# Sparse attention and a routed MoE on one core: transposes of the last batch behind the last load, x of one pair by DMA, scores of one pair in one stretch, and a schedule that reckons with overlapping engines

## The chip, the cores and the metric

The kernel runs on one core of one Trainium2 chip. The metric is the device time of one execution in microseconds (us). Every quoted median is of fast executions; runs of two kernels are compared only where they were taken in turn on one chip. The profile lists TensorE (PE; PEld is its weight load, which overlaps it: 435.9 us beside 656.6 us of matmuls in a span of 664.1 of the kernel before), VectorE (DVE), ScalarE (ACT), GpSimd (POOL) and SyncE (SP), for each of which the program fixes an order of instructions, and 16 DMA engines. In this kernel TensorE's results go to banks of PSUM, from which operations of VectorE and ScalarE read them (in the profile before, `sg` of TensorE by ScalarE, 0.98 us at 65.25, and `vs` by VectorE, 0.28 us at 18.37).

## The reference

```python
# attention: 4 batches x 8 heads, 768 positions, head size 64
k_sum = k.reshape(B, H, nb, 32, D).max(axis=3)         # one summary key per block of 32
v_sum = v.reshape(B, H, nb, 32, D).mean(axis=3)
mask_l = np.abs(pos[:, None] - pos[None, :]) < 16      # local window
a = softmax([scale*q@k.T masked, scale*q@k_sum.T + log(32)])
x = (a @ concat(v, v_sum))                             # -> 3072 tokens x 512
# routed MoE: 8 experts, 512 -> 1024 -> 512
P = np.exp(x @ w_gate - max)
for _ in range(8):                                     # the routing loop
    P /= P.sum(1, keepdims=True) + 1e-09
    P /= P.sum(0, keepdims=True) + 1e-09
    P *= N / E
for e in range(8):
    out += P[:, e:e+1] * (np.maximum(x @ w1[e], 0) @ w2[e])
```

Heads are worked on two at a time: 16 pairs, four to a batch. Pairs 8 to 11 are the third batch, 12 to 15 the fourth.

## The kernel before

All instructions are first put down as units with an engine, an estimated cost and what they depend on. A greedy planner then fixes the order of the whole program, always taking the unit that can start first, by its estimates. PSUM banks are rings in this plan: a unit that opens a bank must wait until all users of the bank's last holder are done. Attention has a ring "a" of three banks and a ring "s" of one double bank.

```python
# Plan.order(), the planner (cut)
            t = max([t0, free.get(e, 0.0)]
                    + [d.end + d.lag + (self.HOP if d.on != e else 0.0) for d in u.deps])
            # ... the unit with the earliest t is taken; among those within 0.02 us, by priority
            u.start, u.end, u.on = t, end, e
            free[e] = end                      # the engine is free when its unit ends
            for b in u.opens:                  # PSUM rings
                ring[b.tag][turn[b.tag] % self.slots[b.tag]] = b
# ...
    BY_DMA = 12        # from pair 12 on keys and queries are transposed by DMA
    X_BY_DMA = 12      # so is x, except for the last pair of a batch
    WHOLE = 10         # from pair 10 on the scores of a pair are one stretch
# ...
        def scores(i):                         # one double bank "s"; whole: two banks "a" more
            sg = at["sg", i, 0] = banks2("sg")
            dst = [[sg[:, j, :] for j in range(2)], None]
            if i >= WHOLE:
                dst[1] = at["sg", i, 1] = [bank("a", "sg1") for _ in range(2)]
            score_mms(i, dst, range(G if i >= WHOLE else HG))

        def to_xT(i, h=None):                  # x of a pair, turned by TensorE
            t = at.pop(("xs", i, h or 0))
            tx = at["tx", i, h] = bank("a", "tx", F16)
            for g in range(G if h is None else HG):
                nc.tensor.transpose(...)

        def x_dma(i):                          # the same by DMA
            nc.sync.dma_start_transpose(out=xT[:, i % PB, t0:t0 + S]..., in_=t...)
# pair_start(i) (cut)
            if i >= BY_DMA:
                for z in range(2):             # keys, queries
                    U["tr", i, z] = add("SP", 1.4, lambda z=z: tr_dma(i, z), ...)
            U["ks", i] = add("DVE", 0.95, lambda: key_max(i), ...)       # largest key of each block
            U["km", i] = add("DVE", 0.23, lambda: key_max_split(i), ...) # -> ksT, for the summary scores ss
# the routing loop (cut)
        for n in range(8):
            rows = add("DVE", 1.65, sink_rows, prev, 0)
            cols = add("PE", 0.1, sink_cols, [rows], 0, opens=[buf], lag=0.1)
            prev = [add("DVE", 0.6, sink_apply, [cols], 0, uses=[buf])]
```

The names in the profile: `tkq` keys and queries turned by TensorE, `sg` scores, `ss` summary scores, `vs` block sums of v, `av` attention output, `xs` its normalised form, `tx` x turned by TensorE, `hps` and `yps` the two layers of expert 0, `lp` the logits, `sink` the column sums of the routing loop.

The softmax here doesn't subtract the row's maximum and nothing guards it: scores larger than these inputs give would overflow.

Of the kernel before, what the change touches and what calls it, by code (L numbers as in the profile page):

```python
# [33 lines left out]
class Plan:  # L34

    HOP = 0.15

    def __init__(self, slots, idle=None):
        self.units, self.slots = [], slots
# [18 lines left out]
    def order(self):  # L58
        free, ring, turn = {}, {t: [None] * n for t, n in self.slots.items()}, {t: 0 for t in self.slots}
        left, n_left, after = [], {}, {}  # L60
        for u in self.units:
            n_left[u] = len(set(u.deps))
            for d in set(u.deps):
                after.setdefault(d, []).append(u)
            if not u.deps:
                left.append(u)
        done = []

        def ready(u):
            t = 0.0  # L70
            for i, b in enumerate(u.opens):
                old = ring[b.tag][(turn[b.tag] + i) % self.slots[b.tag]]
                if old is not None:
                    if any(x.start is None for x in old.users):
                        return None
                    t = max([t] + [x.end + (self.HOP if x.on not in u.eng else 0.0) for x in old.users])
            return t

        while left:
            best = {}  # L80
            for u in left:
                t0 = ready(u)
                if t0 is None:
                    continue
                for e, cost in u.eng.items():
                    t = max([t0, free.get(e, 0.0)]
                            + [d.end + d.lag + (self.HOP if d.on != e else 0.0) for d in u.deps])
                    best.setdefault(e, []).append((t, u, cost))
            picks = []
            for e, c in best.items():  # L90
                t_min = min(t for t, _, _ in c)
                t, u, cost = min((x for x in c if x[0] <= t_min + 0.02), key=lambda x: x[1].prio)
                picks.append((t, t + cost, e, u, cost))
            t, end, e, u, cost = min(picks, key=lambda x: x[:2])
            if self.idle is not None:
                us, fn, until = self.idle
                if until.start is not None:
                    self.idle = None
                while self.idle is not None and t > free.get("PE", t) + us:
                    x = Unit("PE", us, fn, [], 0.0, [Buffer("m")], 0.0)  # L100
                    x.opens[0].users.append(x)
                    t0 = ready(x)
                    if t0 is None or t0 + us > t:
                        break
                    x.start = max(t0, free["PE"])
                    x.end = free["PE"] = x.start + us
                    if x.end > t:
                        break
                    x.on = "PE"
                    ring["m"][turn["m"] % self.slots["m"]] = x.opens[0]  # L110
                    turn["m"] += 1
                    done.append(x)
            u.start, u.end, u.on = t, end, e
            free[e] = end
            for b in u.opens:
                ring[b.tag][turn[b.tag] % self.slots[b.tag]] = b
                turn[b.tag] += 1
            left.remove(u)
            done.append(u)
            for x in after.get(u, ()):  # L120
                n_left[x] -= 1
                if not n_left[x]:
                    left.append(x)
        assert len([u for u in self.units if u.start is None]) == 0
        return done
# [3 lines left out]
def kernel(  # L129
# [10 lines left out]
    nc = tc.nc  # L140

    B, H, S, D = q.shape
    G = S // 128
# [6 lines left out]
    NP = (B * H) // 2  # L150
    PB = H // 2
    SCALE = 1.0 / float(D) ** 0.5
    W = 16
# [4 lines left out]
    VD = D + 1  # L158
    NEH = 3
    BY_DMA = 12  # L160
    X_BY_DMA = 12
    WHOLE = 10
    FILL = {"v0": 1, "S0": 1, "s0": 2, "s1": 1, "s2": 1}

    const = ctx.enter_context(tc.tile_pool(name="const", bufs=1))
# [55 lines left out]
    NB = PB  # L221
# [4 lines left out]
    with tc.manual_schedule():  # L226
# [100 lines left out]
        def tr_dma(i, z):  # L327
# [2 lines left out]
            nc.sync.dma_start_transpose(out=dst.rearrange("c (g t) -> c g t", g=G),  # L330
                                        in_=st[:].rearrange("p g j d -> p (g j d)"))

        def key_max(i):
            r = i % NB
            nc.vector.tensor_reduce(out=ks[r][:, 0, 0:24],
                                    in_=kT[r][:].rearrange("p (n w) -> p n w", w=32),
                                    axis=AX.X, op=ALU.max)
# [44 lines left out]
        def scores(i):  # L382
            sg = at["sg", i, 0] = banks2("sg")
            dst = [[sg[:, j, :] for j in range(2)], None]
            if i >= WHOLE:
                dst[1] = at["sg", i, 1] = [bank("a", "sg1") for _ in range(2)]
            score_mms(i, dst, range(G if i >= WHOLE else HG))

        def scores_1(i):
            sg = at["sg", i, 1] = banks2("sg")  # L390
# [490 lines left out]
        def pair_start(i, prio):  # L881
# [2 lines left out]
            war_q = war_k[:2] + [U.get(("ss", o, 0)), U.get(("ss", o, 1))]  # L884
            ahead = U.get(("S", i - 1, 1 if i > PB else 0))
            if i >= BY_DMA:
                for z in range(2):
                    U["tr", i, z] = add("SP", 1.4, lambda z=z: tr_dma(i, z),
                                        [U["kq"[z], i], U.get(("S", i - 3, 1))] + (war_k, war_q)[z], prio)
                    U["kT", i, z] = add("DMA", 1.7, None, [U["tr", i, z]], prio, lag=2.0)  # L890
            for z in range(0 if i >= BY_DMA else 1 if i < PB else 2):
                buf = Buffer("m" if i < PB else "a")
# [51 lines left out]
        def pair_whole(i, prio):  # L944
# [1 line left out]
                               [U["v", i], U.get(("A", i - NE, 1)), U["vc", i % NE]], prio, lag=5.0 if i < BY_DMA else 3.5)  # L946
            x1 = []
            deps = [U["kT", i, 0], U["kT", i, 1], U.get(("ed", i - 2))]
            bufs = [Buffer("s")] + (2 * [None] if i < WHOLE else [Buffer("a"), Buffer("a")])
            U["S", i, 0] = U["S", i, 1] = add("PE", 0.4 if i < WHOLE else 0.6, lambda: scores(i), deps, prio,  # L950
                                              opens=[x for x in bufs if x is not None])
            U["X", i, 0] = add("ACT", 0.97, lambda: score_exp(i, 0), [U["S", i, 0]], prio, uses=bufs[:1])
            if i < WHOLE:
                buf = Buffer("s")
                U["S", i, 1] = add("PE", 0.4, lambda: scores_1(i), deps, prio, opens=[buf])
                U["X", i, 1] = add("ACT", 0.97, lambda: score_exp(i, 1), [U["S", i, 1], U["X", i, 0]], prio,
                                   uses=[buf])
            else:
                x1 = [add("ACT", 0.53, lambda j=j: score_exp(i, 1, j), [U["S", i, 0], U["X", i, 0]], prio,
                          uses=bufs[1 + j:2 + j]) for j in range(2)]  # L960
                U["X", i, 1] = x1[1]
# [10 lines left out]
            for h in range(2):  # L972
# [3 lines left out]
                                   prio, opens=[buf])  # L976
                U["no", i, h] = add("DVE", 0.75, lambda h=h: normalize(i, h),
                                    [U["A", i, h], U.get(("x", i - 2))], prio, uses=[buf])
            if i >= X_BY_DMA and i % PB < PB - 1:
                U["xt", i] = add("SP", 1.5, lambda: x_dma(i), [U["no", i, 0], U["no", i, 1]], prio)  # L980
                U["x", i] = add("DMA", 1.7, None, [U["xt", i]], prio, lag=2.0)
                return
# [101 lines left out]
        expert0(HS, [U["x", i, 1] for i in range(PB)])  # L1084
        gate(0, [U["x", i, h] for i in range(PB) for h in range(2)], 900)
        for i in range(PB, NP):
            load_pair(i, "" if i == PB else "kqv")
            pair_start(i, 20 + i)
            pair_whole(i, 20 + i)
            if i % PB == PB - 1:  # L1090
                b = i // PB
                xs = [U["x", PB * b + d] for d in range(PB)]
                gate(b, xs, 900 if b < B - 1 else 0)
                expert0(b * S, xs)
                expert0(b * S + HS, xs)
        def transposed():

            r = (NP - 1) % NB
            nc.gpsimd.tensor_copy(out=warm[:, 0:1], in_=kT[r][0:32, 0:1])
            nc.gpsimd.tensor_copy(out=warm[:, 1:2], in_=qT[r][0:32, W:W + 1])  # L1100
            if X_BY_DMA < NP:
                nc.gpsimd.tensor_copy(out=warm[:, 4:5], in_=xT[0:32, PB - 2, (B - 1) * S:(B - 1) * S + 1])
            ve = V_e[(NP - 1) % NE]
            for j in range(2):
                nc.gpsimd.tensor_copy(out=warm[:, 2 + j:3 + j],
                                      in_=ve[64 + 32 * j:96 + 32 * j, G - 2, VD * j:VD * j + 1])

        last[0] = add("POOL", 0.3, transposed, [last[0], U["near", NP - 1]] + [U["kT", NP - 1, z] for z in range(2)]
                      + [U["x", i] for i in range(X_BY_DMA, NP - 1)])
        load("w1n", lambda: load_w1(1), 0.85, 5.0)  # L1110
        load("w2n", lambda: load_w2(1), 0.85, 5.0)
        U["w1", 1], U["w2", 1] = U["w1n"], U["w2n"]
        U["post"] = add("SP", 0.0, pools, [U["lo", b] for b in range(B)] + [last[0]])
        prev = [U["post"]]
        for n in range(8):
            rows = add("DVE", 1.65, sink_rows, prev, 0)
            buf = Buffer("Q")
            cols = add("PE", 0.1, sink_cols, [rows], 0, opens=[buf], lag=0.1)
            prev = [add("DVE", 0.6, sink_apply, [cols], 0, uses=[buf])]
# [201 lines left out]
```

## Time and profile before

| | before |
|---|---|
| median of 3 runs | 666.03 us (665.86 to 666.69) |
| span of the profiled execution | 664.1 us |
| TensorE busy | 656.6 us, 99% |
| VectorE, ScalarE, GpSimd busy | 550.1, 410.9, 199.0 us |
| attention with expert 0, the routing loop, first matmuls of expert 1 | 0 to about 165 us |
| experts 1 to 7 | about 165 us to the end |

A line of TensorE's timeline has the start, the length, the line of the program, the operation with its tiles, and the count. Matmuls overlap each other a little in the profile (six of scores, 0.38 us from 64.66 us, are followed at 64.97), so what a group costs is the distance from its start to the start of the next group, not its length. Where a group starts later than that pace allows, TensorE stood still; I call this a hole. Its size is worked out so from two starts in the trace, and its time is the start of the last matmul before it.

### The profile page before, as it was taken

What the parts mean: (1) busy time and instruction counts of PE and PEld (TensorE: products, weight loads), DVE (VectorE), ACT (ScalarE), POOL (GpSimd) and SP (SyncE); (2) the same over time, 40 slices, a digit from 0 to 9 for tenths busy, and PEclk for the clock granted to TensorE, in tenths of its full rate; (3) what the DMA queues carried; (4) which work ended last, traced back from release to release, by engine and by line L of the source; (5) the groups of instructions that cost most, each with busy time, mean ns of one, the idle gap of its engine ahead of it and who ended that gap; (6) DMA issues with size and microseconds to landing.
All of it is one profiled execution on the core that took longest, in us unless ns stands there. A gap on an engine that the chain in (4) does not pass through costs nothing.

```text
span 664.1 us, 13257 instructions
## 1 busy us (share of the span) xinstructions
PE 656.6 (99%) x5131; PEld 435.9 (66%) x5132; DVE 550.1 (83%) x1036; ACT 410.9 (62%) x769; POOL 199.0 (30%) x257
## 2 busy tenths in 40 slices
PE   8999999999999999999999999999999999999997
PEld 4666666545766666666666666666666666666666
DVE  7899897799988887887779877988778877988776
ACT  6677676556885566556665665555655656556652
POOL 8899522100132222212322222223122213222123
PEclk9999999999999999999999999999999999999999
DMA  9999932700953747373754665373838465335656
GB/s 167 181 145 145 143 70 43 128 1 2 157 96 65 126 75 118 64 128 65 110 97 71 121 91 101 64 127 65 127 64 135 73 96 96 64 64 112 157 134 202
DMA packets 112558, 67.89 MB, mean 102 GB/s; under 512 B 77936, under 2 KB 90480, under 8 KB 112496
## 3 DMA queue, kind: packets, MB, share of 16 engines
q0 software_dynamic: 94816, 57.46, 64.9%
q1 hardware_dynamic: 17152, 9.58, 5.9%
q8 instruction: 40, 0.66, 0.4%
q14 instruction: 22, 0.18, 0.1%
q10 hardware_dynamic: 528, 0.02, 0.0%
HBM read 52.45 MB, written 6.29 MB: 88 GB/s over the span
## 4 chain that ended last, share of the span: by engine, by line
PE 96%; DVE 3%; DMA 1%; issue 0%; ACT 0%; POOLq 0%; DVEq 0%
PE yps L815 22%; PE pA L764 22%; PE pY L815 17%; PE pQ L764 11%; PE hps L211 6%; PE yps L216 6%; PE pR L764 5%; PE sg L347 1%; DMA qst<-in_q_dram 1%; PE av L512 1%; PE vs L357 1%; PE tkq L303 1%; PE av L435 1%; DVE xs L543 1%; PE ss L461 1%; PE av L441 1%
## 5 line engine op out<-in xcount | busy, mean ns | idle before, releaser
L815 PEld LDWEIGHTS <-h 128*128 128x128 f16 x2352 | 230.1, 98 | 88.5 <-issue 1.0
L843 POOL DMA_DIRECT2D out_acc<-y x120 | 101.7, 891 | 372.1 <-ACT y L839 110.3
L839 ACT ACTIVATE y<-pY,P_sb 128x256 f32<-128x256 f32 x168 | 79.8, 477 | 123.3 <-PE pY L815 121.6
L830 DVE SCALAR_TENSOR_TENSOR out_acc<-yps,P_sb,out_acc 128x512 f32<-128x512 f32 x128 | 95.1, 744 | 29.0 <-PE yps L815 29.0
L798 DVE TENSOR_TENSOR h<-h 128x1024 f16<-128x1024 f16 x168 | 109.3, 683 | 1.4
L815 PE MATMUL pY<-w,h 128*128 128x256 f16 x672 | 100.0, 273 | 0.6 <-ACT y L839 0.6
L815 PE MATMUL yps<-w2sum,h 128*128 128x256 f16 x672 | 98.4, 273 | 0.0
L764 PE MATMUL pA<-xT,w 128*128 128x512 f16 x336 | 98.3, 379 | 0.0
L815 PE MATMUL yps<-w,h 128*128 128x256 f16 x672 | 93.3, 273 | 0.0
L830 DVE SCALAR_TENSOR_TENSOR out_acc<-pY,P_sb,out_acc 128x512 f32<-128x512 f32 x84 | 62.8, 748 | 29.1 <-PE pY L815 27.4
L764 PEld LDWEIGHTS <-w 128*128 128x128 f16 x672 | 65.8, 98 | 31.6 <-issue 0.2
L764 PEld LDWEIGHTS <-w1sum 128*128 128x128 f16 x504 | 49.3, 98 | 45.0
L786 DVE CUSTOM_DVE_ANT_0 h<-pQ,snap 128x512 f16<-128x512 f32 x84 | 57.6, 685 | 7.0 <-ACT snap L207 4.3
L786 DVE CUSTOM_DVE_ANT_0 h<-pA,snap 128x512 f16<-128x512 f32 x84 | 57.3, 682 | 4.8 <-PE pA L764 4.8
L202 ACT ACTIVATE h<-pA 128x512 f16<-128x512 f32 x84 | 50.6, 603 | 12.6 <-PE pA L764 12.4
L202 ACT ACTIVATE h<-pR 128x512 f16<-128x512 f32 x84 | 50.1, 596 | 8.0 <-PE pR L764 7.7
L207 ACT COPY pR<-pA 128x512 f32<-128x512 f32 x83 | 47.5, 572 | 7.7 <-PE pA L764 6.9
L815 PE MATMUL pY<-w2sum,h 128*128 128x256 f16 x336 | 50.4, 273 | 0.0
L764 PE MATMUL pA<-xsum,w 128*128 128x512 f16 x168 | 50.0, 379 | 0.0
L764 PE MATMUL pR<-xT,w 128*128 128x512 f16 x168 | 50.0, 379 | 0.0
L764 PE MATMUL pQ<-xsum,w1sum 128*128 128x512 f16 x168 | 50.0, 379 | 0.0
L764 PE MATMUL pA<-xsum,w1sum 128*128 128x512 f16 x168 | 50.0, 379 | 0.0
(150 smaller groups left out, 854.3 us busy)
## 6 DMA issues: line engine op xcount, KB each, us to landing
out_acc<-y POOLq DMA_DIRECT2D x120, 256.0 KB, 3.4
w<-in_moe_w_dram POOLq DMA_DIRECT2D x14, 1024.0 KB, 10.7
out_dram<-out_acc SPq DMA_DIRECT2D x24, 256.0 KB, 2.4
qst<-in_q_dram POOLq DMA_DIRECT2D x32, 96.0 KB, 5.3
vx<-in_v_dram POOLq DMA_DIRECT2D x15, 192.0 KB, 6.2
kst<-in_k_dram POOLq DMA_DIRECT2D x24, 96.0 KB, 5.6
w<-in_moe_w_dram POOLq DMA_DIRECT2D x4, 256.0 KB, 7.6
w<-in_moe_w_dram POOLq DMA_DIRECT2D x2, 512.0 KB, 7.7
```

What stands on the lines that cost most here:

```text
L202: nc.scalar.activation(out=out, in_=in_, func=AF.Relu, bias=0.0, scale=1.0)
L207: (nc.scalar.copy if eng == "ACT" else nc.vector.tensor_copy)(out=out, in_=in_)
L211: nc.tensor.matmul(hp[:, 0:n], lhsT=w1s[e][:, dk, f * 128:(f + 1) * 128], rhs=xT[:, dk, t0:t0 + n], start=(dk == 0), stop=(dk == KD - 1))
L216: nc.tensor.matmul(yp[:, d], lhsT=h[:, f, c * 128:(c + 1) * 128], rhs=w2s[e][:, f, d], start=(f == 0), stop=(f == KF - 1))
L303: nc.tensor.transpose(t[:, g * 128:(g + 1) * 128], st[:, g, :, :].rearrange("p j d -> p (j d)"), ident)
L764: nc.tensor.matmul(dst[:], lhsT=lhsT, rhs=rhs, start=first and k == 0, stop=k == HK - 1, skip_group_check=True)
L786: nc.vector._custom_dve(dve_ops.TENSOR_ADD_SAT, out=ring(e, p, q)[:, q % 2, blk, :], in0=at[src, e, p, q][:], in1=at.pop(("snap", n, e, p, ...
L798: nc.vector.tensor_tensor(out=h[:, :, out_, :], in0=h[:, :, a, :], in1=h[:, :, b, :], op=op)
L815: nc.tensor.matmul(dst[:, d], lhsT=lhsT, rhs=rhs, start=f == 0 and n in (1, 5, 2), stop=f == HF - 1, skip_group_check=True)
L830: nc.vector.scalar_tensor_tensor(out=o, in0=y, scalar=scalar, in1=o, op0=ALU.mult, op1=ALU.add)
L839: nc.scalar.activation(out=at[key][:, d], in_=src, func=AF.Copy, bias=0.0, scale=P_sb[:, t, e:e + 1])
L843: nc.gpsimd.dma_start(out=o, in_=at.pop(("y", e, p, c, key))[:], accum_op=ALU.add)
```

## The change

Its intent is to take work off TensorE (x of pair 10 by DMA: six transposes fewer; the scores of pair 9 in one stretch: one change-over fewer), to keep transposing DMAs out of the way of the loads, and to let the planner know that an operation of VectorE or ScalarE begins before the last one has quite ended (in the kernel before, one of VectorE, 0.68 us from 126.11 us, is followed at 126.71, 0.08 us before its end, and one of ScalarE, 0.59 us from 64.77, at 65.25, 0.11 us before its end).

```diff
@@ the planner
+    OVERLAP = {"DVE": 0.07, "ACT": 0.09}
-            free[e] = end
+            free[e] = end - self.OVERLAP.get(e, 0.0)
@@ constants
-    X_BY_DMA = 12
-    WHOLE = 10
+    X_BY_DMA = {10, 12, 13, 14}
+    WHOLE = {9, 10, 11, 12, 13, 14, 15}
@@ new: two small copies on GpSimd that wait for the last load of q
+        def loads_landed(i):
+            st = at["st", NP - 1, 1]
+            for t in (kT[i % NB][0:32, 0:1], qT[i % NB][0:32, W:W + 1]):
+                nc.gpsimd.tensor_copy(out=t, in_=st[0:32, 0, 0, 0:1])
@@ pair_start
             if i >= BY_DMA:
+                hold = U.get(("tr", i - 1, 1))
+                if i == BY_DMA:
+                    hold = add("POOL", 0.3, lambda: loads_landed(i), [last[0], U["q", NP - 1]] + war_k + war_q, prio)
+                    last[0] = hold
                 for z in range(2):
                     U["tr", i, z] = add("SP", 1.4, lambda z=z: tr_dma(i, z),
-                                        [U["kq"[z], i], U.get(("S", i - 3, 1))] + (war_k, war_q)[z], prio)
+                                        [U["kq"[z], i], U.get(("S", i - 3, 1)), hold] + (war_k, war_q)[z], prio)
@@ all loads of the fourth batch before its first pair
-            load_pair(i, "" if i == PB else "kqv")
+            for n in range(i, NP) if i == BY_DMA else [i] if PB < i < BY_DMA else []:
+                load_pair(n, "kqv")
@@ the routing loop, as the planner reckons it
-            rows = add("DVE", 1.65, sink_rows, prev, 0)
+            rows = add("DVE", 1.5, sink_rows, prev, 0)
... (tests of i against the two sets, where i was compared with a number)
```

More of the change, by code (lines that the diff above doesn't have):

```diff
@@ L384, in scores @@
             dst = [[sg[:, j, :] for j in range(2)], None]
-            if i >= WHOLE:
+            if i in WHOLE:
                 dst[1] = at["sg", i, 1] = [bank("a", "sg1") for _ in range(2)]
-            score_mms(i, dst, range(G if i >= WHOLE else HG))
+            score_mms(i, dst, range(G if i in WHOLE else HG))
         def scores_1(i):
@@ L948, in pair_whole @@
             deps = [U["kT", i, 0], U["kT", i, 1], U.get(("ed", i - 2))]
-            bufs = [Buffer("s")] + (2 * [None] if i < WHOLE else [Buffer("a"), Buffer("a")])
-            U["S", i, 0] = U["S", i, 1] = add("PE", 0.4 if i < WHOLE else 0.6, lambda: scores(i), deps, prio,
+            bufs = [Buffer("s")] + (2 * [None] if i not in WHOLE else [Buffer("a"), Buffer("a")])
+            U["S", i, 0] = U["S", i, 1] = add("PE", 0.4 if i not in WHOLE else 0.6, lambda: scores(i), deps, prio,
                                               opens=[x for x in bufs if x is not None])
             U["X", i, 0] = add("ACT", 0.97, lambda: score_exp(i, 0), [U["S", i, 0]], prio, uses=bufs[:1])
-            if i < WHOLE:
+            if i not in WHOLE:
                 buf = Buffer("s")
@@ L978, in pair_whole @@
                                     [U["A", i, h], U.get(("x", i - 2))], prio, uses=[buf])
-            if i >= X_BY_DMA and i % PB < PB - 1:
+            if i in X_BY_DMA:
                 U["xt", i] = add("SP", 1.5, lambda: x_dma(i), [U["no", i, 0], U["no", i, 1]], prio)
@@ L1100, in transposed @@
             nc.gpsimd.tensor_copy(out=warm[:, 1:2], in_=qT[r][0:32, W:W + 1])
-            if X_BY_DMA < NP:
+            if NP - 2 in X_BY_DMA:
                 nc.gpsimd.tensor_copy(out=warm[:, 4:5], in_=xT[0:32, PB - 2, (B - 1) * S:(B - 1) * S + 1])
@@ L1108 @@
         last[0] = add("POOL", 0.3, transposed, [last[0], U["near", NP - 1]] + [U["kT", NP - 1, z] for z in range(2)]
-                      + [U["x", i] for i in range(X_BY_DMA, NP - 1)])
+                      + [U["x", i] for i in X_BY_DMA])
         load("w1n", lambda: load_w1(1), 0.85, 5.0)
```

## The prediction

> **What bounds the kernel now.** I read the page first, then the waits of TensorE, then the timeline of TensorE, DMA issues and VectorE between 60 and 165 us, because all that the change touches lies before 165 us.
>
> The page, engines and chain:
>
> ```profile
> PE 656.6 (99%) x5131; PEld 435.9 (66%) x5132; DVE 550.1 (83%) x1036; ACT 410.9 (62%) x769; POOL 199.0 (30%) x257
> ...
> PE 96%; DVE 3%; DMA 1%; issue 0%; ACT 0%; POOLq 0%; DVEq 0%
> ```
>
> TensorE works 656.6 of 664.1 us, and the chain that sets the end is TensorE for 96%. Only 7.5 us are left outside it. The waits of TensorE say where:
>
> ```profile
> PE idle L613 <- DVE zeros L632: 1.3, 1, 1.3
> PE tkq L312 <- DMA qst<-in_q_dram: 0.8, 1, 0.8
> PE pY L815 <- ACT y L839: 0.6, 1, 0.6
> PE tkq L300 <- ACT kst L207: 0.3, 1, 0.3
> ```
>
> Three of the four are in the first 8 us, the third is 6 us from the end; another 4 us are the tail behind the last matmul. The windows by stage confirm it (first the stretch, then its length and TensorE's busy time):
>
> ```profile
> 20.00:60.00 40.00, 39.88 (x536) 26.48 (x534) 36.30 (x96) 28.91 (x47) 39.35 (x53) 1.00 2.10 156
> 60.00:117.00 57.00, 56.95 (x609) 36.13 (x607) 48.85 (x134) 39.85 (x74) 25.70 (x41) 1.00 1.12 91
> 117.00:165.00 48.00, 48.00 (x281) 25.47 (x280) 41.49 (x88) 28.81 (x56) 2.94 (x4) 1.00 0.26 45
> 165.00:640.00 475.00, 475.00 (x3292) 321.92 (x3291) 391.62 (x606) 294.27 (x564) 107.71 (x128) 1.00 0.57 98
> ```
>
> From 20 to 640 us TensorE has no hole worth 0.2 us. So there are two currencies here: TensorE work taken away comes off the end one for one; a new wait of TensorE is added one for one, as there is no slack to swallow it. Work moved between the other engines counts only if it makes such a wait.
>
> [...]six transposes of x start at 96.42 and what follows at 96.76, 0.34 us; four 512-column matmuls take 0.86 us. [...]
>
> ```profile
> 126.11 0.68 DVE L718 TENSOR_TENSOR xsum<-xT,xsum 128x1024 f16<-128x1024 f16 x1
> 126.71 0.68 DVE L718 TENSOR_TENSOR xT<-xT 128x1024 f16<-128x1024 f16 x1
> 127.31 0.21 DVE L592 RECIPROCAL crec_sb<-sink 128x8 f32<-128x8 f32 x1
> ```
>
> Operations of 0.68 us follow each other at 0.60 us. [...]
>
> **The change, part by part.**
>
> *x of pair 10 by DMA.* It takes six 128x128 transposes and one copy from PSUM (0.55 us on VectorE or 0.80 on ScalarE) away and adds one transposing DMA on SyncE. The instruction order of the new kernel confirms 78 transposes of x falling to 72. On the path: 6 x 56 ns = 0.34 us off TensorE.
>
> *Scores of pair 9 in one stretch.* The 12 matmuls stay; what goes is one change-over at the end of a stretch. Before:
>
> ```profile
> 64.66 0.38 PE L347 MATMUL sg<-qT,kT 64*128 64x160 bf16 x6
> 64.97 0.51 PE L550 MATMUL tx<-ident_x,xs 128*128 128x128 f16 x6
> ...
> 91.06 0.59 PE L347 MATMUL sg<-qT,kT 64*128 64x160 bf16 x12
> 91.58 1.04 PE L216 MATMUL yps<-w,h 128*128 128x512 f16 x4
> ```
>
> Six take 0.31 us until the next instruction, twelve take 0.52; 2 x 0.31 - 0.52 = 0.10 us saved. TensorE's work thus falls by 0.44 us in all.
>
> *Transposes of the fourth batch behind the last load.* Only pair 12 moves. Before, its keys were issued while loads were still queued:
>
> ```profile
> 66.23 1.32 SPq L330 DMA_TRANSPOSE kT<-kst x1
> 68.01 1.56 SPq L330 DMA_TRANSPOSE qT<-qst x1
> ...
> 78.48 2.25 SPq L330 DMA_TRANSPOSE kT<-kst x1
> ```
>
> They landed 6.7 and 8.1 us later, at 72.9 and 76.1; the other six, issued from 78.48 on, took 2.7 to 6.7 us. The last q load is issued at 73.95 and 75.52 and lands at 82 to 83. In the new order SyncE issues the near values of pairs 10 and 11, then k and q of pair 12, x of pair 10, and pairs 13 to 15. From 82 us on with some 1.7 us an issue and 3 to 5 us to landing, q of pair 12 lands at 87 to 88. When is it needed? Adding up TensorE's instructions in the new order with the intervals measured here puts the scores of pair 12 at about 89.4 us (91.06 before). Margin 1 to 2 us; pairs 13 to 15 are needed at 101, 104 and 113, with far more. So this part should cost and gain nothing; it is a transfer that is hidden in both kernels.
>
> *Overlap in the schedule.* The work is the same, the order changes almost everywhere, and about 24 copies move from ScalarE to VectorE (15 more VectorE instructions, 15 fewer on ScalarE). 24 x 0.69 = 17 us takes VectorE from 83% to some 85%: not a bound. What matters is the routing loop, eight rounds of VectorE, TensorE, VectorE. Before, the schedule reckoned VectorE too slow, and that was slack: the last column sum ends at 159.86, its matmul comes at 163.06, 3.2 us later. In the new order TensorE reaches the last routing matmul 41.6 us after the fourth batch's logits, not 43.5, and VectorE has 40 other operations between the first round and the last column sum, not 32. I counted through the rounds: 1.53 us for the rows, 0.64 for the column step, 0.62 for each other operation. Rounds 3 to 7 keep 0.5 us or more; in round 2 the sum is ready about 0.2 us late; in round 8 it is ready at 42.7 us after the logits against an arrival at 41.8, 0.9 us late. So TensorE could wait 1.1 us in this stretch. The pitches are good to about 0.03 us and there are some 60 steps, so the error is as large as the result; I enter a third of it, 0.37 us.
>
> The sum: 666.03 - 0.44 - 0.15 + 0.37 = 665.8 us. The 0.15 is half of the one true wait in the front that a new order may remove (0.29 us at 20.2 us, where the transposes of x wait for their input).
>
> **The rivals.**
> *A: the routing loop becomes a wait.* For it: the count above, the lost 3.2 us of slack, and the new order placing an h or weight sum between column step and rows in most rounds, which lengthens the loop. Against it: VectorE's free time of 1.4 us in that stretch before, which the new order may use. It would give 666.5 to 667.5 us: 1.1 us to 2 us of wait against 0.44 us saved.
> *B: pair 12 arrives late.* For it: nothing was waited for in this chain before, and now its transposes start 14 to 16 us later, with x of pair 10 and near values of pair 12 (POOL) on the same DMA engines. The key maximum of pair 12 stands in VectorE's fixed order, and a late one holds everything behind it. Against it: 1 to 2 us of margin, and loads that end earlier when no transpose is among them. It would give 666.5 to 668 us.
> *C: only the saved work shows.* No new wait: 665.6 us, and 665.0 with the short waits in the front and near the end (0.3 us at 644.6) gone too. That is the floor, since there is no other idle time that this change touches.
> *D: the longer run of experts 1 to 7 suffers,* as a schedule that reckons with overlap leaves less slack. Against it: TensorE waits 0.0 us for VectorE or ScalarE there, with these at 82% and 62%. I give it 0 to 0.5 us.
>
> **Range and chances.** C's floor is 665.0, and a run to run spread of about 0.4 us (665.86 to 666.69 before) lies on both sides; A and B together make 667.5 a fair upper end. Range 664.9 to 667.5. Two per cent is 13 us, and nothing found here is worth a tenth of that in either direction, so within 2% has 0.985, slower 0.010 (a chain of fixed orders that jams at pair 12 or in the loop), faster 0.005.
>
> **What would show it.** Right: TensorE's busy time falls by about 0.4 us; transposes of x 72; its waits list is the old one or adds less than a microsecond; kT and qT of pair 12 land between 85 and 89 us in under 5.5 us each; the scores of pair 12 follow without a hole. Rival A shows as a gap in front of the routing matmuls (sink) at 125 and 163 us or in front of the first yps of expert 1. Rival B shows as a gap at 87 to 92 us with a DMA as releaser on TensorE, or on VectorE's key maximum. D shows as PE waits for h or y after 170 us. The prediction is wrong if the time is under 664.9, as then idle time existed that I did not see inside the modelled matmul ends, or over 667.5.

Three passages of the recorded text are cut out of it, with the cuts marked, as they state rules that no trace of this case shows. No term of the sum goes with them: it came to 666.03 - 0.44 - 0.15 + 0.37 = 665.8 us. The 56 ns are a sixth of the 0.34 us from 96.42 to 96.76 in the trace, and the three VectorE lines show what the planner's new constant of 0.07 us stands for.

## The result, and the profile after

| | before | after |
|---|---|---|
| median of 6 runs each, in turn | 666.25 us (665.86 to 666.69) | 666.44 us (666.32 to 668.14) |
| ratio of the fast runs, 95% interval | | 1.0007 (0.9994 to 1.002) |
| span of the profiled execution | 664.1 us | 664.7 us |

A ratio is the mean time of one kernel's fast runs over that of the other's of the same rounds, so not quite the ratio of the medians quoted. The time is the same. The measurement lies within the predicted range and 0.64 us above the predicted 665.8.

The page of the changed kernel, engines and chain:

```profile
PE 658.0 (99%) x5125; PEld 435.6 (66%) x5126; DVE 562.8 (85%) x1051; ACT 402.5 (61%) x754; POOL 199.1 (30%) x259
...
PE 95%; DVE 3%; DMA 1%; issue 0%; ACT 0%; SPq 0%; DVEq 0%
```

There are six matmul instructions fewer, 15 more on VectorE and 15 fewer on ScalarE, and yet TensorE is busy for 1.4 us longer. The profile models the ends of matmuls, so that a short hole can count as busy: from 47.5 to 56 us it shows 8.48 busy us of 8.50, where the starts show holes of 0.51 us. The windows by stage of the changed kernel (the stretch, its length and TensorE's busy time, then PEld, DVE, ACT and POOL, the clock, the DMA share and GB/s):

```profile
20.00:60.00 40.00, 39.95 (x524) 26.05 (x523) 35.65 (x97) 30.30 (x52) 39.12 (x52) 1.00 2.14 153
60.00:117.00 57.00, 56.79 (x597) 35.61 (x596) 43.59 (x117) 40.97 (x75) 26.32 (x43) 1.00 1.13 96
117.00:165.00 48.00, 48.00 (x294) 25.52 (x293) 43.08 (x98) 27.85 (x54) 2.45 (x3) 1.00 0.27 45
165.00:640.00 475.00, 475.00 (x3291) 321.81 (x3290) 408.33 (x628) 283.59 (x540) 108.22 (x129) 1.00 0.57 98
```

Experts 1 to 7 are as full as before, with 16.7 us more on VectorE (408.33 against 391.62). That is where VectorE got its additional work: from 20 to 117 us it has 5.9 us less than before. Busy windows hide short holes here, so the starts have to be read. The transposes of x that wait at 20 us start at 20.64 us before and at 20.72 after, and the matmuls behind TensorE's last hole before the tail at 644.87 and 645.60. In between the changed kernel thus needs 0.73 - 0.08 = 0.65 us more. It has 0.54 us less to do there: the 0.44 us that the prediction works out, and 0.10 more, as a stretch of scores begins with a gap of 0.10 us in these traces (those at 64.66, 91.06 and 97.72 us before, and at 39.62, 41.93 and 75.19 after, follow 0.96 us behind the start of four 512-column matmuls, which take 0.86 to 0.88 ahead of other groups) and the changed kernel has one stretch fewer. So it has gained about 1.2 us of new waiting. A list of all holes over 0.12 us between 20 and 120 us finds most of it:

| hole before (us) | | hole after (us) | |
|---|---|---|---|
| 20.19 | 0.28 | 20.37 | 0.20 |
| | | 48.92, before `tx` | 0.16 |
| | | 53.20, between `vs` and `vs` | 0.18 |
| | | 55.47, before `ss` | 0.17 |
| 65.94, before `lp` | 0.21 | | |
| | | 83.08, before `ss` | 0.30 |
| | | 99.48, before `lp` | 0.14 |
| | | 100.27, before `ss` | 0.21 |

The six new ones are 1.16 us together; with the old one at 65.94 gone the sum is 0.95. The first one is not shorter, as 0.07 us of it stand one group earlier in the changed kernel. The trace after 117 us adds 0.05 us at the column sums of 129.3 us and 0.11 at those of 150.5, which makes 1.11; the rest lies in gaps under 0.12 us. What the six wait for is named by the weight loads, which stand ahead of the matmuls. The waits of the weight loads of the changed kernel between 48 and 102 us (line waited for: total, times, longest), and the largest of them in the timelines of PEld and VectorE:

```profile
PEld L468 <- DVE ksT L348: 0.6, 3, 0.3
PEld L364 <- DVE xs L550: 0.2, 1, 0.2
PEld L557 <- DVE xs L550: 0.2, 1, 0.2
PEld L577 <- DVE xs L550: 0.2, 1, 0.2
```
```profile
83.43 0.11 PEld L468 LDWEIGHTS <-ksT 128*128 128x128 bf16 x2 [0.31 <-DVE ksT L348]
```
```profile
81.58 0.95 DVE L342 TENSOR_REDUCE ks<-kT 128x24 bf16<-128x768 bf16 x1
82.45 0.28 DVE L370 TENSOR_TENSOR Ve<-vs,own_n 64x128 bf16<-64x128 f32 x1
82.77 0.48 DVE L374 COPY Ve<-Ve 64x650 bf16<-64x650 bf16 x1
83.17 0.21 DVE L348 TENSOR_TENSOR ksT<-ks,own 128x64 bf16<-128x64 bf16 x1
```

All six end with VectorE: with a key maximum three times and with a normalised `xs` three times. The last operation that the summary scores need comes at 83.17 us, behind a block copy. VectorE works almost without a pause there: 8.00 us of the 8.50 from 47.5 to 56 us, in which three of the holes lie. Before it had 8.09 of 8.50 in this stretch and TensorE no wait for it. At the other holes it is alike: 2.85 of 3.00 us from 81 to 84 us (before 2.71) and 3.78 of 4.00 from 97 to 101 (before 3.84). So it is not a higher load that makes the holes but which operation stands where in a VectorE that is full in both kernels, and when TensorE asks for it. In the kernel before, the key maximum of the same pair 11 came 4.4 us after its `ks` (81.82), behind nine other operations, and nothing waited, as the first summary scores that could need it came at 87.47 us:

```profile
86.25 0.22 DVE L341 TENSOR_TENSOR ksT<-ks,own 128x64 bf16<-128x64 bf16 x1
```
```profile
87.47 0.49 PE L461 MATMUL ss<-qT,ksT 128*128 128x384 bf16 x2
```

After, it comes 3 us earlier, but TensorE asks for it 4 us earlier.

The transposes of pair 12, in the timeline of SyncE of the changed kernel, stand behind the near values of pair 11:

```profile
81.45 0.59 SPq L386 DMA_DIRECT2D Ve<-vx  x1
82.21 1.32 SPq L331 DMA_TRANSPOSE kT<-kst  x1
83.72 1.21 SPq L331 DMA_TRANSPOSE qT<-qst  x1
85.03 1.23 SPq L567 DMA_TRANSPOSE xT<-xs  x1
```

In the trace they land at 85.16 and 87.08 us, x of pair 10 at 89.80, and the scores of pair 12 start at 90.04 without a wait for a DMA.

### The profile page after: what moved, and what is told of

Its sections match the earlier page's. It is cut to its first block, busy times and chain, and to the rows that moved or that the text cites. A ratio compares the mean times of both kernels' runs of the same rounds, so it can differ in the third digit from the quotient of the medians.

```text
span 664.7 us, 13271 instructions
## 1 busy us (share of the span) xinstructions
PE 658.0 (99%) x5125; PEld 435.6 (66%) x5126; DVE 562.8 (85%) x1051; ACT 402.5 (61%) x754; POOL 199.1 (30%) x259
## 4 chain that ended last, share of the span: by engine, by line
PE 95%; DVE 3%; DMA 1%; issue 0%; ACT 0%; SPq 0%; DVEq 0%
PE yps L822 22%; PE pA L771 22%; PE pY L822 17%; PE pQ L771 11%; PE hps L212 6%; PE yps L217 5%; PE pR L771 5%; PE sg L354 1%; DMA kvf<-in_v_dram 1%; PE tkq L304 1%; PE ss L468 1%; PE av L519 1%; PE vs L364 1%; DVE xs L550 1%; DVE ks L342 1%; PE tx L557 1%
## 5 line engine op out<-in xcount | busy, mean ns | idle before, releaser
L822 PE MATMUL pY<-w,h 128*128 128x256 f16 x672 | 100.3, 273 | 0.6 <-ACT y L846 0.6
L822 PE MATMUL yps<-w2sum,h 128*128 128x256 f16 x672 | 100.1, 273 | 0.0
L822 PE MATMUL yps<-w,h 128*128 128x256 f16 x672 | 90.5, 273 | 0.0
L771 PE MATMUL pQ<-xT,w1sum 128*128 128x512 f16 x168 | 50.0, 379 | 0.0
```

What stands on the lines that cost most here:

```text
L771: nc.tensor.matmul(dst[:], lhsT=lhsT, rhs=rhs, start=first and k == 0, stop=k == HK - 1, skip_group_check=True)
L822: nc.tensor.matmul(dst[:, d], lhsT=lhsT, rhs=rhs, start=f == 0 and n in (1, 5, 2), stop=f == HF - 1, skip_group_check=True)
```

## The experiments

Twelve kernels ran, in three calls; each call had its own chip and its own runs of the kernel before (666.46, 666.34 and 666.09 us). All results were correct. After the result my theory was that the parts themselves save what I had worked out, and that the new order of instructions, in which VectorE comes late in six places, eats it. The rivals were the wait for the last load and the DMA traffic of the transposes.

### First call: parts of the change, each with its own plan

**e1, the overlap alone**: the kernel before, with

```diff
+    OVERLAP = {"DVE": 0.07, "ACT": 0.09}
+            free[e] = end - self.OVERLAP.get(e, 0.0)
+            rows = add("DVE", 1.5, sink_rows, prev, 0)
```

> The kernel before with the scheduler's new constants alone (overlap 0.07 and 0.09, rows 1.5); transposes, x of pair 10 and scores of pair 9 as before. TensorE's work is that of before. Theory 1 (the new order's small waits ate the saved 0.44 us): the order alone costs 0.4 to 1.0 us, so 666.6 to 667.2 us where before is 666.25, and TensorE shows new short holes between 20 and 120 us. Rival 2 (the transposes behind the last load cost it): no change, 666.2 within 0.2. Rival 3 (the 0.44 us were never saved, the rest is chance): 666.2 within 0.2.

Measured: 669.02 us, ratio 1.0032 (1.002 to 1.0044). The waits of this kernel between 48 and 97 us, an issue in its SyncE timeline, and VectorE where that transfer is used:

```profile
DVE ks L342 <- DMA kT<-kst: 1.3, 1, 1.3
...
PE ss L468 <- DVE Ve L370: 0.6, 1, 0.6
PE av L448 <- DMA Ve<-vx: 0.5, 1, 0.5
```
```profile
79.12 4.43 SPq L331 DMA_TRANSPOSE kT<-kst  x1
```
```profile
89.56 0.95 DVE L342 TENSOR_REDUCE ks<-kT 128x24 bf16<-128x768 bf16 x1 [1.04 <-DMA kT<-kst]
```

The keys issued at 79.12 took 10.4 us to land, at 89.53. VectorE, whose order is fixed, stood for them, and TensorE lost 0.76 and 0.38 us behind it (89.94 and 91.57 us), with 0.69 us more at 51.27 for near values that landed late and 0.44 at 81.43 for VectorE. This is the kind of wait that rival B of the prediction feared, but for a later pair and in a kernel that lacks the new wait, to which rival B had put it down. Four of the six runs took 668.9 to 669.5 us and two 667.1 to 667.2; what makes these 2 us I do not know.

**e2, all but the overlap**: the changed kernel, with

```diff
-    OVERLAP = {"DVE": 0.07, "ACT": 0.09}
+    OVERLAP = {}
```

> The changed kernel without the overlap (constants emptied, rows kept at 1.5): late transposes, x of pair 10 by DMA, scores of pair 9 in one stretch. Theory 1: the saved 0.44 us show, 665.7 to 666.0 us. Rival 2: the late transposes stay, so does the wait, 666.3 or more, with a hole before the scores or summaries of pairs 11 and 12 (83 to 92 us). Rival 3: 666.2 within 0.2.

Measured: 667.45 us (667.37 to 667.60), ratio 1.0016 (1.0003 to 1.0029). My expectation failed: without the overlap the time should have fallen below the kernel before. TensorE waits at 64.3 us for `xs` (0.71 us) and at 65.2 us for the key maximum (0.67), and has a third hole of 0.34 us at 67.2.

**e3, the changed kernel without the wait for the last load**, in its plan too, and with the old order of loads:

```diff
-                hold = U.get(("tr", i - 1, 1))
-                if i == BY_DMA: ...
+                hold = None
-            for n in range(i, NP) if i == BY_DMA else [i] if PB < i < BY_DMA else []:
-                load_pair(n, "kqv")
+            load_pair(i, "" if i == PB else "kqv")
```

> The changed kernel with the transposes of the fourth batch issued as before, each as soon as its own loads are in. Theory 1: 666.3 to 666.7 us, the holes between 20 and 60 us stay, since they lie before any of these transposes. Rival 2: 665.7 to 666.0 us. Rival 3: 666.2 within 0.2.

Measured: 665.99 us (665.89 to 666.99), ratio 0.9997 (0.9985 to 1.0009). Its keys of pair 12 are issued at 69.57 us and land after 7.1 us, at 76.64, still early enough. Four holes over 0.15 us are left between 45 and 100 us, 0.16, 0.19, 0.16 and 0.28 us; the two of the changed kernel at 99.48 and 100.27 us are missing.

**e4, the two work-saving parts alone**: the kernel before with `X_BY_DMA = {10, 12, 13, 14}` and `WHOLE = {9, ..., 15}`.

> The kernel before with x of pair 10 by DMA and the scores of pair 9 in one stretch, and nothing else. Theory 1 and rival 2 alike: 0.44 us less work on TensorE and no new wait, 665.7 to 665.9 us. Rival 3: 666.2 within 0.2, with TensorE's starts showing no gain of 0.44 us between 60 and 120 us.

Measured: 669.75 us (668.57 to 670.04), ratio 1.0046 (1.0034 to 1.0058). This is the clearest miss: the two parts that save 0.44 us cost 3.3 us. The waits of TensorE between 60 and 70 us and the windows there, of e4:

```profile
PE tx L557 <- DVE xs L550: 0.6, 1, 0.6
PE ss L468 <- DVE ksT L348: 0.5, 1, 0.5
```
```profile
62.00:65.00 3.00, 2.50 (x33) 1.71 (x31) 2.93 (x8) 1.24 (x3) 3.00 (x5) 1.00 2.31 149
65.00:68.00 3.00, 2.32 (x47) 1.90 (x48) 2.81 (x10) 1.98 (x4) 3.00 (x4) 0.94 2.37 150
68.00:71.00 3.00, 3.00 (x17) 1.82 (x16) 1.39 (x5) 1.46 (x3) 3.00 (x5) 0.50 2.64 143
```

They are the same two holes as in e2, 0.71 and 0.66 us, on a VectorE that has 2.93 of 3.00 us of work, and the third of 0.34 us follows here too. Then the granted clock falls, to 0.50 from 68 to 71 us (0.94 in the stretch before): 17 matmuls there where e2 has 28. What decides it does not show: in the two stretches before, TensorE was busy for 2.50 and 2.32 us here and for 2.54 and 2.27 in e2, which has the same three holes and keeps 1.00, and of the five executions of e4 itself three have a mean clock of 0.997 and two of 0.999 and 1.000.

```profile
68.00:71.00 3.00, 3.00 (x28) 2.06 (x27) 2.52 (x7) 1.95 (x4) 3.00 (x5) 1.00 2.57 143
```

So my theory in its first form fell: e2 and e4 have the old planner, which does not reckon with overlap, and wait even longer. Two questions were open: whether the wait for the load does anything, and whether the parts or the plan made anew from them cost the time.

### Second call: one thing moved, all else in place

**e5, the changed kernel in its own order, without the wait**: the two copies of `loads_landed` are replaced by `pass`; every other engine keeps its order.

> The changed kernel with the planned order of every engine left as it is; only the two small copies with which GpSimd waits for the last load are not issued, so the transposes of pair 12 may start as soon as their place in SyncE's order comes. Theory (the order of instructions decides, the wait itself is hidden): the same time as the changed kernel, 666.4 within 0.3 us, the same three waits for the key maximum at 55.5, 83 and 100 us. Rival (the wait costs the half microsecond): 665.9 or less, with one of the holes gone.

Measured: 666.47 us (666.27 to 668.05), ratio 1.0004 (0.999 to 1.0018); the changed kernel had 666.44 in another call. The six new holes are the same within 0.02 us. The wait itself is never waited for: SyncE issues the keys of pair 12 at 82.36 us here and at 82.21 with the wait, and they land at 85.21 and 85.16. What the part does, it does through the plan, which now puts these transposes behind the near values.

**e6, the changed kernel with earlier key maxima**: the finished order, with each `key_max_split` moved up to one VectorE operation behind its `key_max`:

```diff
+        order = plan.order()
+        for i in range(PB, NP):
+            km, lo = U["km", i], max(order.index(U["ks", i]), order.index(U["ss", i - NB, 1]))
+            if order.index(km) > lo + 1:
+                ...                      # take it out, put it back behind the next VectorE unit
-        for u in plan.order():
+        for u in order:
```

> The changed kernel with nothing moved but VectorE's key maximum of each pair, which is issued one VectorE operation after its keys are ready and no longer behind normalisations and block copies. TensorE's order stays. Theory (late key maxima are what ate the saving): the holes in front of the summaries at 55.5, 83.1 and 100.3 us, 0.17 + 0.30 + 0.21 us, go, and no other appears: 665.8 us, 0.6 less than the changed kernel. Rival (those holes only take the place of waits that come anyway): 666.3 to 666.6.

Measured: 666.38 us (666.23 to 666.90), ratio 0.9998 (0.9986 to 1.001). The rival was right. The hole at 55.5 us is gone. The one at 83.1 stays at 0.30, as there the block copy was the one operation in between anyway. The one at 100.3 stays at 0.21 us although the key maximum now comes at 99.55 us and not at 100.23. The weight loads of the summary scores between 98 and 101 us, first in the changed kernel, then in e6:

```profile
PEld L468 <- DVE ksT L348: 0.2, 1, 0.2
```
```profile
PEld L468 <- DVE xs L550: 0.2, 1, 0.2
```

Where the wait for the key maximum went, the next one showed: 0.2 us for the normalisation, which by the plan's rings reads its PSUM bank before the summary scores may have it. In this stretch VectorE is as good as full (3.78 of 4.00 us in the changed kernel), and moving one operation ahead moved another back.

**e7, e4 with earlier key maxima** (the edit of e6 on e4).

> The kernel before with x of pair 10 by DMA and the scores of pair 9 in one stretch alone (run as e4 at 669.75), with the key maxima moved as in e6. Theory[...]: without the second hole, 0.5 to 0.66 us, the granted clock stays at 1.00 and 2.2 to 2.7 us come back: 667.0 to 667.5. Rival (the clock drop has nothing to do with that hole[...]): 669.0 to 669.3.

Measured: 669.75 us (668.92 to 671.61), ratio 1.0052 (1.0036 to 1.0069). Missed again: the hole before `ss` is not gone but 0.89 us long at 67.75, behind one of 0.69 at 64.58 and one of 0.65 at 65.89 us. A further 1.0 us of holes stands between 174 and 184 us, in e7 as in e4; in the longest, 0.40 us, TensorE waits for a copy of ScalarE. Its profiled execution, of 668.92 us, kept the clock at 1.00 with these holes, so that here holes of this size came without a lower clock; the three executions of 670.4 to 671.6 us have a mean granted clock of 0.997, the three of 668.9 to 669.1 us 0.999 or 1.000, and 0.3% of 667 us is 2.0 us. So the larger part of the loss needs no lower clock.

**e8, e3 with earlier key maxima** (the edit of e6 on e3).

> The changed kernel without the wait for the last load in the plan (run as e3 at 665.99), with the key maxima moved as in e6. Theory: its hole at 55.5 us (0.16) goes, those at 48.9 and 53.2 stay: 665.8 us, the best of all so far, 0.6 under the kernel before. Rival: 666.0 or more.

Measured: 665.81 us (665.78 to 666.58), ratio 0.9992 (0.9979 to 1.0004). This is the lowest median of all, with f1 (665.82, another call) beside it, but its interval includes 1: a version that beats both kernels is not shown. The profiled execution, at 666.58 the slowest of the five, lacks all three holes, at 48.9, 53.2 and 55.5 us, and has one of 0.19 us at 51.8 and one of 0.43 at 84.0 instead. e6 of the same call differs from it by the wait and what it does to the plan, and took 0.57 us longer; e3 against the changed kernel points the same way. With the profile's few tenths of difference between executions I take this as a hint, not as shown.

### Third call: the two parts in the old order, without a new plan

Here the plan of the kernel before is made first, and only then is the one unit replaced. This separates a part from the plan that is made anew because of it.

**f1, x of pair 10 by DMA:**

```diff
         for u in plan.order():
-            if u.fn is not None:
+            if u is U["xt", 10]:
+                x_dma(10)
+            elif u.fn is not None and u is not U["x", 10]:
                 u.fn()
```

> The kernel before with its plan made first and left as it is; afterwards only the six transposes of x of pair 10 and their copy are struck out and the transposing DMA of x issued in their place. Nothing else moves. Theory (the saved work is real and counts one for one; in e4 it was the plan made anew that lost 3.3 us): 0.34 us less than the kernel before, about 666.0, with no new hole over 0.15 us, and x of pair 10 lands at 92 to 95 us, well before the logits at 102. Rival (the transposing DMA itself costs the time, by DMA traffic or a late x): 666.5 or more, with a hole near 89 to 103 us.

Measured: 665.82 us (665.63 to 666.24) against 666.09, ratio 0.9993 (0.9981 to 1.0006). The difference of the medians, 0.27 us, is about what was expected, though the interval includes none; the traces show it better. TensorE at this place, first the kernel before, then f1:

```profile
88.44 0.49 PE L461 MATMUL ss<-qT,ksT 128*128 128x384 bf16 x2
88.77 0.50 PE L550 MATMUL tx<-ident_x,xs 128*128 128x128 f16 x6
89.11 0.51 PE L357 MATMUL vs<-vx,m_blk 128*128 128x128 bf16 x6
```
```profile
88.78 0.49 PE L461 MATMUL ss<-qT,ksT 128*128 128x384 bf16 x2
89.11 0.51 PE L357 MATMUL vs<-vx,m_blk 128*128 128x128 bf16 x6
```

This execution of f1 was 0.33 us later by 20 us already (its hole there stands at 20.52, not at 20.19), and so it is at 88.78 against 88.44. Then six transposes are missing, and both kernels start `vs` at 89.11 and still run level at 644.87 us. Between 66 and 645 us the part saves 0.33 us, no more and no less, and no new hole appears. x lands after 5.0 us, at 93.85, before the last pair of its batch is turned by TensorE at 96.4, so nothing waits for it. Here work taken off TensorE came off one for one, as the order was left alone.

**f2, the scores of pair 9 in one stretch:**

```diff
+        U["S", 9, 0].fn = lambda: scores_9()      # twelve matmuls, into "s" and two banks of "a"
+        U["S", 9, 1].fn = None
+        U["X", 9, 1].fn = lambda: [score_exp(9, 1, j) for j in range(2)]
```

> As f1, but only the scores of pair 9 are joined: the second six matmuls are issued right behind the first six, into two other PSUM banks, in the old order of everything else. Theory: 0.1 us less work, but the two extra banks may have to be waited for once, so 666.2 to 666.6. Rival (the joined stretch is what jams e4): a hole of over 0.5 us at 62 to 68 us, 667 or more.

**f3, both**, that is f1 and f2 in one kernel.

> f1 and f2 in one: the two work-saving parts of the change in the old order. Theory: the whole 0.44 us, 665.8 to 666.0. Rival: 669 as in e4, if the parts themselves and not the plan made anew cause the two holes at 64 and 65 us and the lower clock.

Measured: f2 668.13 us (668.12 to 669.17), ratio 1.0028 (1.0014 to 1.0042); f3 667.82 us (667.70 to 667.97), ratio 1.0023 (1.0011 to 1.0036). The difference of the two, 0.31 us, is the x of pair 10 once more. The rival was right as to the holes: joining the scores in this place costs 2 us. TensorE there, before and in f3:

```profile
62.68 0.38 PE L347 MATMUL sg<-qT,kT 64*128 64x160 bf16 x6
62.99 0.36 PE L435 MATMUL av<-vx,em 128*128 128x65 bf16 x6
63.19 0.34 PE L441 MATMUL av<-Ve,Ee 128*128 128x130 bf16 x3
63.36 0.50 PE L357 MATMUL vs<-vx,m_blk 128*128 128x128 bf16 x6
```
```profile
62.70 0.59 PE L347 MATMUL sg<-qT,kT 64*128 64x160 bf16 x12
63.88 0.36 PE L435 MATMUL av<-vx,em 128*128 128x65 bf16 x6 [0.60 <-DVE xs L543]
64.08 0.34 PE L441 MATMUL av<-Ve,Ee 128*128 128x130 bf16 x3
65.30 0.51 PE L357 MATMUL vs<-vx,m_blk 128*128 128x128 bf16 x6 [0.88 <-DVE xs L543]
65.65 1.02 PE L216 MATMUL yps<-w,h 128*128 128x512 f16 x4
66.51 0.50 PE L550 MATMUL tx<-ident_x,xs 128*128 128x128 f16 x6
67.66 0.49 PE L303 MATMUL tkq<-ident,kst 128*128 128x128 bf16 x6 [0.65 <-DVE xT L207]
```

The twelve scores take two of the three "a" banks at 62.7 us, and ScalarE, whose order I had left alone, reads these only at 67.2 us: it stood for 2.57 us before that for `yps`, which TensorE issues behind the matmuls that wait here. Until then `av`, `vs`, `tx` and `tkq` share the third bank, each waiting for VectorE to empty it: 0.66 + 1.05 + 0.81 = 2.52 us. Between the holes at 20 and at 645 us f3 takes 2.10 us more than f1, which is these 2.52 less the 0.20 saved and less f1's hole of 0.22 at 66.3, which is gone. The 2.52 us are what one bank for four groups cost in this trace. The clock stays at 1.00 throughout, so no lower clock is needed for the 2 us.

This does not say that joined scores must cost 2 us. The planner knows the rings and puts them elsewhere: in the changed kernel at 70.43 us, with the next group at 70.95.

```profile
70.43 0.59 PE L354 MATMUL sg<-qT,kT 64*128 64x160 bf16 x12
70.95 0.51 PE L304 MATMUL tkq<-ident,kst 128*128 128x128 bf16 x6
```

That is 0.52 us for twelve against twice 0.31, the 0.10 us that were to be saved, and the gap of 0.10 us before a stretch comes once, not twice. But a plan made anew has another order round the place, and so it came to the holes of e2 and e4 with one estimate of VectorE and to the six small ones of the changed kernel with the other. What joined scores are worth within the changed kernel's own order was not run.

**f4, f3 with two units of TensorE set back**: the transposes of x that wait at 20.2 us behind the next two matmuls, the logits that wait at 65.9 us behind the next four.

> f3 with two units of TensorE set back: the first-batch transposes of x that wait at 20.2 us (0.28) go behind the next two hidden-layer matmuls, the logits that wait at 65.9 us (0.21) behind the next four. Theory (only TensorE's work and its holes count): 0.44 + 0.28 + 0.21 = 0.9 us under the kernel before, 665.3 to 665.5. Rival: the waits turn up behind the moved units, 665.8 to 666.0.

Measured: 668.16 us (667.77 to 668.52), ratio 1.0028 (1.0015 to 1.004). Missed, as the rival had it and on top of f3's loss: the hole at 20.2 us turns up in front of the matmuls that were moved up, and longer, 0.41 us; the one at 65.9 us is not in f3 at all. The matmuls that were to fill it wait for an x copied by ScalarE:

```profile
20.76 0.48 PE L211 MATMUL hps<-xT,w 128*128 128x384 f16 x2 [0.24 <-ACT xT L207]
```

## Why the prediction was right or wrong

The time lay in the range and in the class that had 0.985, and that is in part luck: the range was 2.6 us wide, nothing found could have moved the time by 2%, and the forecast gain of 0.2 us did not show. Of the four terms of the sum one came out as worked out, one had been put at half its size, one did not come and one was a third of an event that hardly came; the largest item was not among them.

| term | predicted | measured |
|---|---|---|
| x of pair 10 by DMA | -0.34 | -0.33 (f1, trace) |
| scores of pair 9 in one stretch | -0.10 | -0.20 (0.52 for 0.62, and one gap of 0.10 fewer) |
| the wait at 20.2 us | -0.15 | 0 (0.28 before; 0.07 + 0.20 after; 0.28 in e5, of the same order) |
| routing loop | +0.37 | +0.16 (0.05 and 0.11) |
| other new waits of TensorE, 20 to 120 us | 0 | +0.95 (1.16 new, 0.21 gone) |
| sum | -0.2 | +0.6 |

The measured terms make +0.58 us, and the two traces differ by +0.65 between the holes at 20 and 645 us. The medians differ by less, 0.19 us; their interval, -0.4 to +1.3 us, includes both figures. The first 20 us alone vary by some 0.3 us between executions of one order: the hole there stands at 20.19 us in the kernel before and at 20.52 in f1. So neither a loss nor the predicted gain of 0.2 us is shown by the times; that the gain was eaten is read from the traces, and e5 has the holes of the changed kernel once more.

Two readings of the prediction were off. "From 20 to 640 us TensorE has no hole worth 0.2 us" overlooks 0.28 at 20.19 and 0.21 at 65.94, and the gap before a stretch of scores was not counted. Of its signs of being right, the 72 transposes of x, the landing of pair 12 (after 2.9 and 3.4 us) and its scores without a hole came; TensorE's busy time rose by 1.4 us instead of falling by 0.4.

**What bounds the kernel** was right: TensorE, with removed work and new waits counting one for one. f1 shows the first, e1 to e4 and f2 the second.

**The step that failed** is the one on the overlap in the schedule: "The work is the same, the order changes almost everywhere ... takes VectorE from 83% to some 85%: not a bound. What matters is the routing loop". The number was right, 85%, and the conclusion was not. An average of 85% does not tell that VectorE is full to 94 or 95% in the short stretches at 47.5 to 56, 81 to 84 and 97 to 101 us (8.00 of 8.50, 2.85 of 3.00, 3.78 of 4.00). It was about as full there before, without a wait; what differs is the order of VectorE and TensorE, and the new one leaves TensorE waiting a few tenths each time. I had counted through VectorE in the routing loop alone, where I expected the loss, and not through the attention stage before it. With it went the half-sentence on the transposes, that this part "should cost and gain nothing": its transfer is hidden, as said, and its wait costs nothing (e5), but it changes the plan, which by e3 and e8 may cost half a microsecond.

**Rival A** was mis-sized. I had counted 1.1 us of waiting, 0.2 in round 2 and 0.9 in round 8. The trace has 0.05 us in round 2, 0.11 in round 5 and none in the last one, whose column sums start at 164.22 us.

**Rival B** did not come in the changed kernel. The predicted landing of q of pair 12, 87 to 88 us, was 87.08; the scores needed it at 90.04 and not at 89.4. The last load of q landed at 79.72 us, with no transpose issued by then, and at 83.04 in the kernel before, with five. There, from 60 to 84 us, the transposes took no longer than other transfers: 6.5 and 6.7 us from issue to landing (medians), the loads and near values 6.5 to 7.6. The eight of the fourth batch took 2.7 to 8.1 us in the kernel before and 2.7 to 4.3 in the changed one, behind the last load of q. That keys can come late is shown by e1, where some landed after 10.4 us and VectorE stood for 1.04.

**Rival C**, only saved work, is what f1 does; the changed kernel does not reach it. **Rival D** did not come: the starts show no hole over 0.1 us from 165 to 640 us in either kernel, with VectorE at 408 of 475 us there. The danger was not empty: e4 and e7 have 1.0 us of holes from 174 to 184 us.

**What the prediction did not think of** is that each part of such a change is not an edit of a program but a new input of a greedy planner. All five kernels that the planner made from some of the parts (e1 to e4 and the changed kernel itself) have holes in the attention stage that the kernel before has not, and they lie, in two calls, from 666.0 to 669.8 us: a spread of 3.8 us, where the parts are worth some 0.5. Why the planner, with its estimates, comes to these orders was not followed up.

## What to carry to other kernels

Where a planner sets the order, test a saving twice, once in the old order with only that unit replaced and once with a new plan; the first tells what the part is worth, the second what the order happens to cost. When a matmul group is made larger, count the PSUM banks it holds and what their last reader waits for (2.52 us of waiting in f3), not only the change-overs it saves (0.20 us). And a mean load of an engine says nothing on stretches of 3 us: read the starts in those before calling it no bound.
